# Linear attention followed by a SoLU layer: the leftover keys of two heads in row tiles, key sums and numerators in two shared banks

## The chip, the cores and the metric

The kernel runs on one core of one Trainium2 chip. The metric is the device time of one execution in microseconds, lower is better; a comparison uses the median of several runs. PE is the matrix engine, DVE, ACT and POOL the vector, scalar and GpSimd engines, SP the queue that issues all DMAs here.

## What is computed

Eight batches of eight heads, 576 tokens each, head width 64, go through a linear attention with 256 features; the 512 columns of the eight heads then go through a layer with a softmax gate and a layer norm.

```python
def phi(x):                                   # w_phi is 64 x 128
    proj = np.einsum('bhsd,df->bhsf', x, w_phi)
    proj = proj - np.max(np.abs(proj), axis=-1, keepdims=True)
    return np.concatenate([np.exp(proj), np.exp(-proj)], axis=-1)
q_p, k_p = phi(q), phi(k)
kv = np.einsum('bhsf,bhsd->bhfd', k_p, v)
z = np.sum(k_p, axis=2)
num = np.einsum('bhsf,bhfd->bhsd', q_p, kv)
den = np.einsum('bhsf,bhf->bhs', q_p, z)[..., None] + 1e-06
x = (num / den)                               # to 4608 rows of 512
h = x @ w_in                                  # 512 x 1024
e = np.exp(h - h.max(-1, keepdims=True)); solu = h * e / (e.sum(-1, keepdims=True) + 1e-9)
out = layer_norm(solu) * g_ln @ w_out         # 1024 x 512
```

## The kernel before

A unit `u` (16 of them) is four heads of one batch: two pairs, `sub` 0 and 1, of two heads `j` each. The host writes the keys and values of the two pairs one behind the other: 512 tokens of pair 0, its last 64, the last 64 of pair 1, 512 tokens of pair 1. So a unit has three groups `g` of token blocks of 128: four blocks of pair 0, one mixed block (`g` = 1, rows 0 to 63 belong to pair 0 and 64 to 127 to pair 1), four blocks of pair 1.

For the keys of a group, PE multiplies them with `w_phi` (`k_rows`, `k_mid`; tile pjk, both heads side by side as two row tiles of 64 rows), DVE takes the largest magnitude m and subtracts it, and ACT takes the exponentials of both signs `s` (tile ek, 128 tokens x 2 signs x 128 features). Unit 0 skips the subtraction on DVE: ACT takes the exponentials from PSUM, 128 columns at a time. Queries get their features fq in one of two ways; pjq, dT and pq are PE's part of that.

A visit (`visit`, one for each pair, V0 to V31) sums keys times values: for each head and sign it accumulates, over five blocks of tokens, ek (weights, split into two column tiles of 64 features) times the values rv with a column of ones, 65 columns. The fifth block is the mixed one, with the values of the other pair replaced by zeros (tile vz, cleared once by POOL, its halves loaded by `v_half_load`). All four sums stand in one PSUM bank; `kv_ev` copies them out (260 columns) to kvf. From the fifth visit on (`JOIN = 4`) PE runs the numerators of the previous pair, fq times kvf (`q_num`, 18 products in two column tiles for each sign), ahead of the key sums, into two banks of their own; `q_ev` copies these out with two instructions (390 and 195 columns) to E. For the first four pairs `q_num` is a step of its own. Then ACT, DVE, POOL and DVE again make the quotient y (rc, recip, `divide`, `x_turn`), and SP writes it to DRAM (dx).

The second part reads the quotients of a batch back (xT, from dx), splits them into high and low parts (ah by ACT, al and S by POOL) and runs Strassen-like products of 128x128 by 512 columns, U and h, then the gate, and the last product, o. It can start when the four pairs of batch 0, that is V0 to V4, are through. Its weights w_in and w_out come as 1 MB pieces wraw, which ACT (whi, the casts wb_h and wt_h, the scaling by g) and DVE (two instructions, the second joins the two halves) and POOL turn into high and low parts during the first 75 us.

The order of all steps is written out: `SEQUENCE` lists their numbers, and each engine executes its own in that order. PSUM has six banks of tag a, which everything here but h shares. A helper records each instruction, so all have line 275.

Of the kernel before, what the change touches and what calls it, by code (L numbers as in the profile page):

```python
# [8 lines left out]
F32 = mybir.dt.float32  # L9
# [22 lines left out]
JOIN = 4  # L32
# [10 lines left out]
    rk=3, rkm=2, rv=3, m=4, e=6, eh=2, kf=2, qr=2, qh=4, q4=2, m4=2, E=2, rc=2,  # L43
# [6 lines left out]
    ("rkm", 512), ("e", 5120), ("q4", 4608), ("qr", 2304), ("qh", 2304), ("E", 2376), ("kf", 1040),  # L50
# [236 lines left out]
def linear_attention_then_moe(ctx: ExitStack, tc, qT, qT2, kT, v, w_phi, w_in, g_ln, w_out, out):  # L287
# [51 lines left out]
    for t in v_half:  # L339
        nc.gpsimd.memset(t, 0.0)  # L340
# [279 lines left out]
    def visit(st, sub, before):  # L620

        kv = st["kv", sub] = bank("a", [P, 512], "kv")
        if before:
            q_num(*before)
# [132 lines left out]
    def q_ev(st, sub, i):  # L757
        if i == 0:
            st["E", sub] = sb("E", [P, 9, Z2], name="E")
# [585 lines left out]
```

## Time and profile before

| | us |
|---|---|
| median of 3 runs | 626.7 (625.62 to 628.13) |
| the profiled execution | 624.85 |
| its span, first to last instruction | 623.1 |
| PE busy | 610.3 (98%) |
| PE weight loads busy | 523.1 (84%) |
| DVE, ACT, POOL busy | 469.6, 460.7, 431.1 |

The granted clock of PE is full in every slice of the span. Matmuls overlap, so PE's busy time says where it works and not how fast; the distance from one start to the next does. DMA moves 166 GB/s on average, most in the first 30 us.

### The profile page before, as it was taken

The page shows a single profiled execution, that of the slowest core. Times are in us where ns is not written, and L with a number is a line of the kernel's source. Part 1 is how long each engine was busy: PE and PEld are TensorE (multiplying, and loading weights), DVE is VectorE, ACT ScalarE, POOL GpSimd, SP SyncE. Part 2 cuts the span into 40 slices and gives each one's busy share as a digit, 9 for nine tenths or more (in the row PEclk, how much of TensorE's full clock was granted, in tenths as well). Part 3 has the DMA queues.
Part 4 walks back from the last instruction along what each step waited for, and adds up shares of the span by engine and source line. Part 5 has one row for each costly group of instructions (what it writes and reads, how often), then busy time and mean ns, then how long its engine had stood idle before and what let it go on. Part 6 is the DMA issues. An engine that isn't in the chain of part 4 may idle for free.

```text
span 623.1 us, 19130 instructions
## 1 busy us (share of the span) xinstructions
PE 610.3 (98%) x7596; PEld 523.1 (84%) x7596; DVE 469.6 (75%) x1027; ACT 460.7 (74%) x872; POOL 431.1 (69%) x468
## 2 busy tenths in 40 slices
PE   7998999999999999999999999999999999999997
PEld 7887788888888888888888888888888888888886
DVE  5998899788779777887886699988878853454540
ACT  6998899588758977397686768787885685465662
POOL 0687898787659763867685676657886685586832
PEclk9999999999999999999999999999999999999999
DMA  8977435754557554636744455556543444456331
GB/s 273 362 232 234 122 124 164 212 148 138 173 152 180 170 188 150 177 86 181 229 157 131 155 163 183 174 169 179 168 139 107 139 153 126 126 144 201 125 133 69
DMA packets 100201, 103.33 MB, mean 166 GB/s; under 512 B 50448, under 2 KB 73232, under 8 KB 99600
## 3 DMA queue, kind: packets, MB, share of 16 engines
q1 hardware_dynamic: 100112, 102.11, 53.7%
q8 instruction: 60, 0.98, 0.7%
q14 instruction: 29, 0.24, 0.1%
HBM read 64.85 MB, written 37.22 MB: 164 GB/s over the span
## 4 chain that ended last, share of the span: by engine, by line
PE 92%; ACT 3%; POOL 1%; DMA 1%; issue 1%; DVE 1%; SPq 0%; ACTq 0%; POOLq 0%
PE o L275 32%; PE U L275 15%; PE h L275 12%; PE num L275 11%; PE kv L275 11%; PE pjk L275 6%; PE pq L275 4%; ACT ek L275 1%; DMA rawk<-in_k 1%; POOL al L275 1%; ACT fq L275 1%; PE dT L275 1%; ACT whi L275 0%; PE pjq L275 0%; POOL S L275 0%
## 5 line engine op out<-in xcount | busy, mean ns | idle before, releaser
L275 PE MATMUL o<-w_out_h,uhs 128*128 128x512 f32 x280 | 110.4, 394 | 0.0
L275 PE MATMUL o<-w_out_l,uhs 128*128 128x512 f32 x280 | 109.2, 390 | 0.0
L275 PE MATMUL o<-w_out_h,uls 128*128 128x512 f32 x280 | 109.0, 389 | 0.0
L275 POOL TENSOR_TENSOR uls<-uTs,uhs 128x1024 fp32r<-128x1024 f32 x35 | 83.7, 2390 | 35.6 <-ACT uhs L275 15.7
L275 ACT ACTIVATE ek<-ek 128x512 f32<-128x512 f32 (+1 forms) x150 | 86.7, 604 | 13.9 <-DVE ek L275 13.3
L275 PEld LDWEIGHTS num<-kvf,fq 128*64 128x64 f32 x2304 | 69.8, 137 | 9.5 <-issue 3.9
L275 PE MATMUL kv<-rv,ek 128*64 128x65 f32 x2048 | 76.6, 222 | 0.7 <-DMA rv<-in_v 0.5
L275 ACT ACTIVATE fq<-fq 128x640 f32<-128x640 f32 (+1 forms) x104 | 69.1, 678 | 7.5 <-DVE fq L275 7.1
L275 PE MATMUL num<-kvf,fq 128*64 128x65 f32 x2304 | 74.1, 222 | 0.0
L275 PEld LDWEIGHTS kv<-rv,ek 128*64 128x64 f32 x2048 | 70.8, 138 | 1.5 <-ACT ek L275 0.6
L275 POOL TENSOR_TENSOR blk<-blk,m 128x1152 f32<-128x1152 f32 x26 | 55.5, 2133 | 19.1 <-DVE m L275 19.1
L275 ACT ACTIVATE eu<-h,nm 128x1024 f32<-128x1024 f32 x36 | 40.2, 1117 | 37.7 <-DVE nm L275 29.0
L275 POOL TENSOR_TENSOR y<-E,rc 128x512 f32<-128x512 f32 x64 | 42.8, 690 | 32.6 <-DMA dx<-y 16.3
L275 POOL TENSOR_TENSOR al<-S,ah 128x512 fp32r<-128x512 f32 x36 | 46.8, 1300 | 26.8 <-ACT ah L275 26.6
L275 DVE SCALAR_TENSOR_TENSOR eu<-h,eu 128x1024 f32<-128x1024 f32 x36 | 43.6, 1211 | 25.6 <-ACT eu L275 22.7
L275 PEld LDWEIGHTS o<-w_out_h,uhs 128*128 128x128 f32 x280 | 52.5, 188 | 12.2 <-issue 0.4
L275 PEld LDWEIGHTS o<-w_out_h,uls 128*128 128x128 f32 x280 | 52.6, 188 | 11.1
L275 PEld LDWEIGHTS o<-w_out_l,uhs 128*128 128x128 f32 x280 | 52.6, 188 | 10.6
L275 DVE STREAM_TRANSPOSE blk<-pq 128x320 f32<-128x320 f32 (+1 forms) x104 | 44.5, 456 | 19.8 <-PE pq L275 19.6
L275 DVE TENSOR_REDUCE m<-pjk 128x4 f32<-128x512 f32 (+1 forms) x96 | 49.4, 541 | 10.5 <-PE pjk L275 10.1
L275 POOL TENSOR_TENSOR al<-xT,ah 128x512 fp32r<-128x512 f32 (+1 forms) x36 | 37.6, 1044 | 25.6 <-ACT ah L275 24.0
L275 DVE STREAM_TRANSPOSE ub<-eu 128x1024 f32<-128x1024 f32 x35 | 43.2, 1235 | 15.8 <-ACT eu L275 8.8
(116 smaller groups left out, 1561.6 us busy)
## 6 DMA issues: line engine op xcount, KB each, us to landing
du<-ub SPq DMA_DIRECT2D x35, 512.0 KB, 2.9
uTs<-du SPq DMA_DIRECT2D x140, 128.0 KB, 3.1
dx<-y SPq DMA_DIRECT2D x32, 288.0 KB, 2.4
out<-os SPq DMA_DIRECT2D x35, 256.0 KB, 3.1
rv<-in_v SPq DMA_DIRECT2D x32, 264.0 KB, 3.8
rawk<-in_k SPq DMA_DIRECT2D x32, 256.0 KB, 4.1
xT<-dx SPq DMA_DIRECT2D x64, 128.0 KB, 3.2
rawq<-in_q SPq DMA_DIRECT2D x26, 288.0 KB, 3.4
```

The lines of the kernel that those rows point to most:

```text
L275: return self.tc.keep_in_program_order(method(*args, **kwargs))
```

## The change

The host now writes the mixed block by heads instead of by pairs: for the keys, pair `sub` stands on rows 64 sub to 64 sub + 63 of the input and the two heads' 64 leftover tokens side by side, so that after `k_mid` rows 0 to 63 of ek are head 0 and rows 64 to 127 head 1, with the pairs in the two halves of the tile; the values likewise. A new step `visit_mid` (Vm, "the mid" below) multiplies them: for each sign two products, one for each head, in row tiles of 64 rows by 128 features, each head into a bank of its own. The padded tiles, their clearing and their second load are gone.

The visit itself takes up the two banks of its mid, has four blocks of tokens instead of five, and puts the numerators of the previous pair into the same two banks: half of them and head 0's sums into the first, the rest and head 1's sums into the second. Two copies (455 and 390 columns, tile KE) take the place of three; the first visit's copy 130 each. Every visit but the first takes numerators along; only the last pair's have a step of their own.

```diff
-JOIN = 4
...
+    def visit_mid(st, sub):
+        kv = st["kv", sub] = [bank("a", [P, 512], "kv") for _ in range(2)]
+        e, rv = st["kf", 1, None], st["rv", 1]
+        for s in range(2):
+            for j, r in enumerate(HEADS):
+                nc.tensor.matmul(
+                    block(kv[j], KV_AT[j] + s), lhsT=e[r, sub, s], rhs=rv[r, sub, :Z1], start=s == 0, stop=False,
+                    skip_group_check=True,
+                )
     def visit(st, sub, before):
-        kv = st["kv", sub] = bank("a", [P, 512], "kv")
-        if before:
-            q_num(*before)
+        kv = st["kv", sub]
         tiles = [(st["rv", 2 * sub][:, t], [st["kf", 2 * sub, j][:, t] for j in range(2)]) for t in range(4)]
-        tiles.append((st["vz"][:, sub], [st["kf", 1, None][:, j] for j in range(2)]))
         for j in range(2):
+            if before:
+                q_num(*before, kv, j, False)
             for s in range(2):
-                o = kv[:, (2 * j + s) * Z1 : (2 * j + s + 1) * Z1]
+                o = block(kv[j], KV_AT[j] + s)
                 for i, (rv, e) in enumerate(tiles):
                     for r in HEADS:
-                        nc.tensor.matmul(o[r], lhsT=e[j][:, s, r], rhs=rv[:, j, :Z1], start=i == 0, stop=i == 4)
+                        nc.tensor.matmul(
+                            o[r], lhsT=e[j][:, s, r], rhs=rv[:, j, :Z1], start=False, stop=i == 3,
+                            skip_group_check=True,
+                        )
...
-    def kv_ev(st, sub):
-        st["kvf", sub] = sb("kf", [P, 4, Z1], name="kvf")
-        nc.scalar.copy(out=st["kvf", sub].rearrange("p a f -> p (a f)"), in_=st["kv", sub][:, : 4 * Z1])
+    def visit_ev(st, sub, i, n):
+        if i == 0:
+            KE[n] = sb("KE", [P, sum(NB) * Z2], name="KE")
+        first, size = (0, NB[i]) if n else (KV_AT[i], 2)
+        evict(KE[n], KE_AT[i] + first, st["kv", sub][i], first, size)
...
+    kt[..., 512 : 512 + P] = k[..., 512:, :].transpose(0, 1, 2, 5, 3, 4).reshape(B, 2, P, P)
...
 SEQUENCE = (
-    0, 2, 110, 3, 177, 87, 90, 76, 88, 20, 180, 91, 181, 92, 78, 95, 93, 182, 94, 183, 83, 111, 79, 97, 112,
...
```

`SEQUENCE` is new throughout. Three places show it.

PE, the visit V14 of the kernel before, at 211.9 us of its trace. num and kv are column tiles, pjk and pq row tiles, o and h use the whole array; a count is of products.

```order
L275 MATMUL o<-w_out_h,uls 128x512
L275 MATMUL num<-kvf,fq 64x65 x36
L275 MATMUL kv<-rv_69,ek 64x65 x8
L275 MATMUL kv<-vz_71,ek 64x65 x2
L275 MATMUL kv<-rv_69,ek 64x65 x8
L275 MATMUL kv<-vz_71,ek 64x65 x2
...
L275 MATMUL pjk<-wph,rawk 128x128 x8
L275 MATMUL pq<-hq,w_hh 128x320 x2
```

The same engine in the new order, the visit V13 with its mid ahead and V14's mid behind it (kv<-vz is the mid, kv<-KE the numerators).

```order
L273 MATMUL U<-wt_h_623,al 128x512
L273 MATMUL kv<-vz_70,ek 128x65 x4
L273 MATMUL pq<-hq,w_hh 128x320 x2
L273 MATMUL pq<-hq,w_ll 128x320 x2
L273 MATMUL pq<-lq,w_hh 128x320 x2
L273 MATMUL kv<-KE,fq 64x65 x20
L273 MATMUL kv<-rv_68,ek 64x65 x16
L273 MATMUL kv<-KE,fq 64x65 x16
L273 MATMUL kv<-rv_68,ek 64x65 x16
L273 MATMUL kv<-vz_71,ek 128x65 x4
L273 MATMUL pq<-hq,w_hh 128x256 x2
```

The padded products have left the visit, numerators and key sums alternate by bank, and the mid stands with other row-tile products ahead of the visit that it belongs to.

SP at the start: the order before, as far as the first piece of w_in, then the new order's first six rows.

```order
L275 DMA rawq_148<-in_q 128x512
L275 DMA wph<-in_w_phi 128x128
L275 DMA rawk<-in_k 128x128 x2
L275 DMA rawk<-in_k 128x512
L275 DMA vz_70<-in_v 64x132
L275 DMA wraw_162<-in_w_in 128x2048
```

```order
L273 DMA wraw_137<-in_w_in 128x2048
L273 DMA rawk<-in_k 128x128
L273 DMA wph<-in_w_phi 128x128
L273 DMA rawk<-in_k 128x128
L273 DMA rawk<-in_k 128x512
L273 DMA rawq_185<-in_q 128x512
```

A piece of w_in, 1 MB, has moved from the seventh place to the first, ahead of the first keys and w_phi.

ACT at the start: the order before, as far as its first work on w_in, then the new one (m is the negated maximum, ek the exponentials of unit 0's keys).

```order
L275 ACTIVATE m<-m 128x2
L275 ACTIVATE ek<-pjk,m 128x128 x4
L275 ACTIVATE ek<-ek 128x2x128
L275 ACTIVATE m<-m 128x4
L275 ACTIVATE ek<-pjk,m 128x128 x4
L275 ACTIVATE m<-m 128x4
L275 ACTIVATE whi<-wraw_162 128x1024
```

```order
L273 ACTIVATE whi<-wraw_137 128x1024
L273 CAST wb_h<-w_3_141 128x1024
L273 ACTIVATE m<-m 128x2
L273 ACTIVATE ek<-pjk,m 128x128 x2
L273 ACTIVATE m<-m 128x4
```

The work on that piece now stands ahead of the first exponentials; wb_h waits for DVE, which has to join the halves first.

## Rows read from the trace of the kernel before

**Rows 1.** The page's head and part 1: busy us (share of the span) xinstructions.

```profile
span 623.1 us, 19130 instructions
...
PE 610.3 (98%) x7596; PEld 523.1 (84%) x7596; DVE 469.6 (75%) x1027; ACT 460.7 (74%) x872; POOL 431.1 (69%) x468
```

**Rows 2.** The page's part 4, the chain that ended last, by engine.

```profile
PE 92%; ACT 3%; POOL 1%; DMA 1%; issue 1%; DVE 1%; SPq 0%; ACTq 0%; POOLq 0%
```

**Rows 3.** Busy time by stage: us, each engine busy (xinstructions), clock, DMA share, GB/s.

```profile
8.50:49.70 41.20, 37.72 (x808) 33.90 (x806) 39.21 (x71) 40.66 (x110) 26.60 (x20) 1.00 0.86 299
49.70:66.60 16.90, 14.05 (x322) 12.47 (x319) 14.07 (x25) 14.49 (x30) 11.65 (x8) 1.00 0.76 216
66.60:618.90 552.30, 551.89 (x6433) 470.41 (x6431) 414.13 (x925) 401.94 (x725) 391.59 (x433) 1.00 0.52 154
```

**Rows 4.** Chain that ended last, 205 to 229 us: start us, us, what.

```profile
211.88 2.25 PE num L275 x72
214.13 2.33 PE kv L275 x80
216.46 1.09 PE pjk L275 x16
...
218.35 1.57 PE h L275 x6
...
225.36 1.36 PE h L275 x6
```

**Rows 5.** The same chain, 248 to 251 us.

```profile
249.20 0.89 PE pjk L275 x16
```

**Rows 6.** Timeline of weight loads, windows 211.79:211.895 and 216.385:216.48: start, us, engine, what.

```profile
211.81 0.20 PEld L275 LDWEIGHTS num<-kvf,fq 128*64 128x64 f32 x4 [0.35 <-ACT ek L275]
...
216.39 0.19 PEld L275 LDWEIGHTS pjk<-wph,rawk 64*128 64x128 f32 x2
```

**Rows 7.** Timeline of all engines, 201.0 to 201.5 us.

```profile
201.07 0.19 PEld L275 LDWEIGHTS pq<-hq,w_hh 64*128 64x128 f32 x2
201.08 0.38 PE L275 MATMUL pq<-hq,w_hh 64*128 64x256 f32 x2
201.18 0.19 PEld L275 LDWEIGHTS pq<-hq,w_ll 64*128 64x128 f32 x2
201.30 0.28 PE L275 MATMUL pq<-hq,w_ll 64*128 64x256 f32 x2
```

**Rows 8.** Timeline of all engines at the start.

```profile
0.72 0.39 SPq L275 DMA_DIRECT2D rawq<-in_q  x1
...
6.13 0.20 ACT L275 ACTIVATE m<-m 128x2 f32<-128x2 f32 x1 [4.13 <-DVE m L275]
...
8.50 0.20 ACT L275 ACTIVATE m<-m 128x4 f32<-128x4 f32 x1 [0.69 <-DVE m L275]
...
9.85 1.11 ACT L275 ACTIVATE whi<-wraw 128x1024 f32<-128x1024 f32 x1
...
15.92 1.21 DVE L275 SCALAR_TENSOR_TENSOR w<-whi,w 128x1024 uint32<-128x1024 uint32 x1
...
18.79 1.17 ACT L275 CAST wb_h<-w 128x1024 fp32r<-128x1024 f32 x1
```

**Rows 9.** DMAs of tile wraw, issue to landing, us.

```profile
DMA to landing us min/median/max: 5.6/7.0/10.9
```

**Rows 10.** Timeline of all engines ahead of the first U.

```profile
62.79 0.68 ACT L275 CAST ah<-xT 128x512 fp32r<-128x512 f32 x1
...
63.66 1.34 ACT L275 ACTIVATE w<-w,gcol 128x512 f32<-128x512 f32 x2
...
66.62 0.47 PE L275 MATMUL U<-wb_h,ah 128*128 128x512 f32 x1
```

**Rows 11.** Groups of ACT's instructions: busy us, mean ns.

```profile
L275 ACT COPY E<-num 128x390 f32<-128x390 f32 x32 | 16.3, 509 | 15.5 <-PE num L275 13.8 <-POOL sa L275 1.4
...
L275 ACT COPY E<-num 128x195 f32<-128x195 f32 x32 | 11.2, 349 | 1.7 <-PE num L275 1.5
```

More of the change, by code (lines that the diff above doesn't have):

```diff
@@ L315, in linear_attention_then_moe @@
     v_full = [const.tile([P, 4, 2, Z2], F32, name=f"rv{i}") for i in range(NRV)]
-    v_half = [const.tile([P, 2, 2, Z2], F32, name=f"vz{i}") for i in range(NVZ)]
+    v_mid = [const.tile([P, 2, Z2], F32, name=f"vz{i}") for i in range(NVZ)]
     wph = const.tile([P, F], F32, name="wph")
@@ L532, in v_load, with v_mid_load @@
         nc.sync.dma_start(out=rv[:, :nt], in_=v[st["b"], st["qd"], :, t0 : t0 + nt])
[L534 to L538 removed]
+    def v_mid_load(st):
+        vm = st["rv", 1] = v_mid[plan.slot[st["u"], "rv", 1]]
+        nc.sync.dma_start(out=vm, in_=v[st["b"], st["qd"], :, 4])
     def two_banks(name):
@@ L618, in k_exp_direct, with block, blocks @@
                 )
+    KV_AT, NUM_AT, KE_AT, NB = (0, 4), (2, 0), (0, 7), (7, 6)
+    def block(x, i):
+        return x[:, i * Z2 : i * Z2 + Z1]
+    def blocks(x, i, n):
+        return x[:, i * Z2 : (i + n) * Z2].rearrange("p (b f) -> p b f", f=Z2)
+    def visit_mid(st, sub):
[7 more added lines that the diff above has]
+                )
@@ new lines, in evict, with kv_of, num_of @@
+    def evict(out, o, x, i, n):
+        nc.scalar.copy(out=blocks(out, o, n)[:, :, :Z1], in_=blocks(x, i, n)[:, :, :Z1])
+    KE = {}
+    def visit_ev(st, sub, i, n):
[3 more added lines that the diff above has]
+        evict(KE[n], KE_AT[i] + first, st["kv", sub][i], first, size)
+    def kv_of(n, j, s):
+        return block(KE[n], KE_AT[j] + KV_AT[j] + s)
+    def num_of(n):
+        return blocks(KE[n + 1], NUM_AT[0], 9)
@@ L736, in q_exp, with q_num @@
         nc.scalar.activation(out=f[:, :, s], in_=f[:, :, 1], func=AF.Exp, scale=1.0 - 2.0 * s)
-    def q_num(st, sub):
-        odd, kvf = st["b"] % 2, st["kvf", sub]
-        po = st["num", sub] = [bank("a", [P, 512], "num") for _ in range(2)]
+    def q_num(st, sub, po, half, first):
+        odd, n = st["b"] % 2, 2 * st["u"] + sub
         lone = 0 if odd else 8
@@ L748, in run, with last_num, last_ev @@
                     f = st["qf", sub, c][:, j, s, k * D - Q0[c] : (k + 1) * D - Q0[c]]
-                    nc.tensor.matmul(o[HEADS[h]], lhsT=f, rhs=kvf[:, 2 * j + s], start=s == 0, stop=s == 1)
-        for p in range(4):
-            for j in range(2):
-                i = 2 * (p % 3) + j
-                run([(2 * p + odd + h, j, h) for h in range(2)], po[p // 3][:, i * Z2 : i * Z2 + Z1])
-        run([(lone, h, h) for h in range(2)], po[1][:, 2 * Z2 : 2 * Z2 + Z1])
-    def q_ev(st, sub, i):
+                    nc.tensor.matmul(
+                        o[HEADS[h]], lhsT=f, rhs=kv_of(n, j, s), start=first and s == 0, stop=s == 1,
+                        skip_group_check=True,
+                    )
+        todo = [[(2 * p + odd + h, j, h) for h in range(2)] for p in (2 * half, 2 * half + 1) for j in range(2)]
+        if half == 0:
+            todo.insert(0, [(lone, h, h) for h in range(2)])
+        for i, b in enumerate(todo):
+            run(b, block(po[half], NUM_AT[half] + i))
+    def last_num(st, sub):
+        po = st["num"] = [bank("a", [P, 512], "num") for _ in range(2)]
+        for half in range(2):
+            q_num(st, sub, po, half, True)
+    def last_ev(st, i, n):
         if i == 0:
-            st["E", sub] = sb("E", [P, 9, Z2], name="E")
-        n = 6 - 3 * i
-        out = st["E", sub][:, 6 * i : 6 * i + n, :Z1]
-        nc.scalar.copy(out=out, in_=st["num", sub][i][:, : n * Z2].rearrange("p (b f) -> p b f", b=n)[:, :, :Z1])
+            KE[n] = sb("KE", [P, sum(NB) * Z2], name="KE")
+        evict(KE[n], KE_AT[i] + NUM_AT[i], st["num"][i], NUM_AT[i], 5 - i)
     def den_eps(st, sub):
         st["rc", sub] = sb("rc", [P, NBLK], name="rc")
-        den = st["E", sub][:, :, 32:33].to_broadcast([P, 9, 2])
+        den = num_of(2 * st["u"] + sub)[:, :, 32:33].to_broadcast([P, 9, 2])
         nc.scalar.activation(
@@ L776, in divide @@
     def divide(st, sub):
-        e, rc = st["E", sub].rearrange("p b (h f) -> p (b h) f", h=2)[:, :, :32], st["rc", sub]
+        e, rc = num_of(2 * st["u"] + sub).rearrange("p b (h f) -> p (b h) f", h=2)[:, :, :32], st["rc", sub]
         y = st["y", sub] = sb("y", [P, S], name="y")
-        for n, o, h in ((slice(0, 16), y[:, :512], 4), (slice(16, 18), y[:, 512:], 2)):
+        for n, o, h in ((slice(2, 18), y[:, :512], 4), (slice(0, 2), y[:, 512:], 2)):
             nc.gpsimd.tensor_tensor(
@@ L800, in keys_values @@
     def keys_values(n):
-        return [(n // 2, "kve", n % 2)]
+        return [(n // 2, "kve", n % 2, i) for i in range(2)]
     def features(n):
@@ L831, in linear_attention_then_moe @@
             else:
-                for i in range(2):
-                    add(("vl", g, i), "sync", dma(n * 256), z - 3.5, v_half_load, (i,), [("vl", g, 0)] if i else [("abs", "vz")],
-                        () if i else [("vz", ("rv", g))], [("rv", g)])
+                add(("vl", g), "sync", dma(n * 512), z - 3.5, v_mid_load, (), (), [("vz", ("rv", g))])
             add(("kp", g), "tensor", 224 if g == 1 else 4 * 224, z, k_mid if g == 1 else k_rows,
@@ L854, in linear_attention_then_moe @@
             n = 2 * u + sub
-            joined = n >= JOIN
             z = 4.0 + 4.5 * sub
-            cost = 20 * BLOCK
+            cost = 16 * BLOCK
             pu, ps_ = (n - 1) // 2, (n - 1) % 2
-            feats = [(2 * sub, 0), (2 * sub, 1), (1, None)]
-            after = [("ke", *x, 1) for x in feats] + [("vl", 2 * sub), ("vl", 1, 1)]
-            tiles = [("e", *x) for x in feats] + [("rv", 2 * sub), ("rv", 1)]
-            alloc, early = [("a", ("kv", sub))], {}
-            if joined:
+            feats = [(2 * sub, 0), (2 * sub, 1)]
+            both = [("kv", sub, i) for i in range(2)]
+            add(("Vm", sub), "tensor", 2 * BLOCK, z, visit_mid, (sub,), [("ke", 1, None, 1), ("vl", 1)],
+                [("a", x) for x in both], [("e", 1, None), ("rv", 1)])
+            after = [("Vm", sub)] + [("ke", *x, 1) for x in feats] + [("vl", 2 * sub)]
+            tiles = [("e", *x) for x in feats] + [("rv", 2 * sub)] + both
+            early = {(u, "kve", sub, 0): 16 * BLOCK / 2}
+            if n:
                 after += [("abs", x) for x in features(n - 1)] + [("abs", x) for x in keys_values(n - 1)]
-                tiles += [("abs", (pu, "f", ps_, c)) for c in range(2)] + [("abs", (pu, "kf", ps_))]
-                alloc += [("a", ("abs", (pu, "num", ps_, c))) for c in range(2)]
-                early = {(pu, "qv", ps_, c): cost + 6 * BLOCK * (1 - c) for c in range(2)}
+                tiles += [("abs", (pu, "f", ps_, c)) for c in range(2)] + [("abs", ("KE", n - 1))]
+                early = {(u, "kve", sub, 0): 16 * BLOCK}
                 cost += 18 * BLOCK
-            add(("V", sub), "tensor", cost, z, visit, (sub, (states[pu], ps_) if joined else None), after, alloc, tiles,
-                early)
-            add(("kve", sub), "scalar", act(4 * Z1, True), z, kv_ev, (sub,), [("V", sub)], [("kf", ("kf", sub))],
-                [("kv", sub)])
+            add(("V", sub), "tensor", cost, z, visit, (sub, (states[pu], ps_) if n else None), after, (), tiles, early)
+            for i in range(2):
+                add(("kve", sub, i), "scalar", act(460 - 66 * i, True), z, visit_ev, (sub, i, n),
+                    [("V", sub)] + ([("kve", sub, 0)] if i else []), () if i else [("KE", ("abs", ("KE", n)))],
+                    [both[i], ("abs", ("KE", n))])
         if not qsp:
```

40 lines of the change are left out of this document (16 added, 24 removed), and 270 rows, old and new, of the table SEQUENCE.

## The prediction

> **What bounds the kernel now.** I read the page first: of a span of 623.1 us PE is busy 610.3 [rows 1]. Busy PE is no proof that PE is the bound, so the chain that ended last came next: 92% of it is PE, 3% ACT [rows 2]. The busy time by stage then says where that holds [rows 3]. From 66.6 to 618.9 us PE lacks 0.4 us of 552, while DVE, ACT and POOL have 130 us and more to spare: there only what PE executes counts. Ahead of 66.6 us it is another kernel: ACT lacks 0.5 us of 41 between 8.5 and 49.7, and PE stands still for 3.5.
>
> So the change is worth what it takes from PE's stream after 66.6 us, plus what it does to the time of the first U matmul, 66.62 us. The profiled execution took 624.85 us, 1.75 over its span; the median of the runs is 626.7. I add the difference to both.
>
> **PE's prices.** Every fp32 product is two instructions on each of two tiles side by side; I call what two tiles do together a pass. Three forms of the array occur: whole (128\*128: o, U, h, dT), column tiles (128\*64: num, kv), row tiles (64\*128: pjk, pjq, pq). From the chain around the visit at 211.9 us [rows 4]:
> - column tiles: kv x80, 40 passes in 2.33 us, 0.058 each;
> - row tiles, 128 columns streamed: 8 passes in 0.89 us where row tiles ran before them [rows 5], 0.111 each;
> - a change of form: the same pjk x16 take 1.09 behind column tiles, so 0.20 to enter row tiles; h x6 take 1.57 behind row tiles and 1.36 in a run of its own form, 0.21 to enter the whole array; num x72 take 2.25, of which 36 passes are 2.10, 0.15 to enter column tiles [rows 4, 5].
>
> **The leftover keys.** Each of the 32 visits now spends 8 of its 40 kv passes on the padded fifth block: 8 x 0.058 = 0.466 us. The mid puts four products there, two per sign, head 0 on rows 0 to 63 and head 1 on rows 64 to 127: 4 passes. The price of such a pass is in no row: it streams 65 columns as kv does, but loads weights of 128 columns as pjk does. Its ends are 0.058 (streaming limits) and 0.16 (a load of 0.11 and a stream of 0.05, half of pjk's, one after the other). What decides is the weight load. Right behind a change of form, four loads of 64 columns begin within 0.085 us, but only two of 128 columns within 0.09 [rows 6]; and in pq, entered from another form, the second pair of loads starts 0.11 after the first, and the second pair of matmuls 0.22 after the first, a load and a stream of 0.11 each [rows 7]. So a pair of 64x128 loads takes about 0.11 us and a 64-column load half of that. In kv load and stream are equally long, in pjk too; in the mid the stream is halved and the load is not. I take 0.111: 4 x 0.111 = 0.444 us instead of 0.466, 32 x -0.022 = -0.7 us. The ends: 32 x (0.234 - 0.466) = -7.4 and 32 x (0.64 - 0.466) = +5.6 us.
>
> The page "TensorEngine Tiling (Array Packing)" of the Trainium skill, section Theoretical Speedup, gives a contraction of at most 64 a factor of up to two; the mid by it would be the -7.4.
>
> **Changes of form.** Counted over PE's whole order, before against now: into the whole array 43 and 43, into column tiles 35 and 33, into row tiles 44 and 57. Half the mids (16) follow a product of the whole array and precede another row-tile group, as in the order shown above: there the visit, entered from the whole array before, now is entered from row tiles, and what followed it has to be entered all the same. Cost: 13 x 0.20 - 2 x 0.15 = +2.3 us. Nine mids stand right ahead of another form; their last pass ends after 65 columns, not 128: 9 x -0.05 = -0.5. Nothing hides these, since PE is the bound.
>
> **Evictions and banks.** Three evictions of 260, 390 and 195 columns become two of 455 and 390. The rows have 0.51 us for 390 and 0.35 for 195 [rows 11], so 0.16 per 195 columns: 0.40 + 0.51 + 0.35 before, 0.56 + 0.51 now, 0.19 us of ACT less a visit. ACT has 150 us free in that stage [rows 3]: nothing. Without that cover it would be 32 x 0.19 in favour. A visit holds two banks of six instead of three, but from the mid on; PE waits nowhere for a bank after 66.6 us, so nothing, either way. Numerators now wait for the key sums that share their bank, up to 2.3 us longer; behind them stand only the divisions, whose output is wanted a batch later. The first batch is the exception, and belongs to the start. Sixteen fewer DMAs on SP's queue and no clearing of padded tiles on POOL: nothing, neither stands in the chain.
>
> **The start.** Ahead of the first U, PE executes the same numbers of pjk, pjq, pq, num and kv products, 24 mids for 48 padded products and six more dT: at the prices above 51.5 us against 51.7. U starts at 66.62, so 15 us are lost there now, to ACT's queue mostly. That queue is rearranged: the first DMA becomes 1 MB of w_in, and whi and the cast of wb_h stand ahead of every exponential. It is issued at about 0.72 us, where rawq is now; the eight 1 MB pieces land 5.6 to 10.9 us after their issue [rows 8, 9]. Nothing is queued ahead of this one, so I take 6: landed at 6.7, whi 1.0, DVE's join 1.2, wb_h 0.95, and the exponentials begin at 9.9. By then ACT has done 3.1 us of work in the kernel before (from 6.13, less 0.69 of idling [rows 8]), and 2.0 in the new one: 1.1 behind. Ahead of the first ah stand four multiplications by g (two take 1.34 [rows 10]), one exponential less, three evictions less: about 1.8 more. Against that ACT idles 2.4 us between 49.7 and 66.6 [rows 3]. The first ah, at 62.79 [rows 10], moves by 1.1 + 1.8 - 2.4 = 0.5, and the POOL work on w_in starts earlier. The last numerators of the first batch now leave PE at their visit's end, up to 2.3 us later, and division, transpose and DMA have that much less until the first ah; some of what they have now is spent in ACT's queue, where ah waits its turn. I take the start as even, with bounds of -2 (the 2.4 of idle ACT gone) and +4.5 (below).
>
> **Sum.** -0.7 + 2.3 - 0.5 + 0 = +1.1 us: a span of 624.2, an execution of 626.0, and 626.7 + 1.1 = **627.8 us** for the median. By its own bounds, the start's, this case lies between 625 and 630.
>
> **The rivals.**
> 1. The mid's passes are limited by streaming, 0.058 each: -7.4 + 2.3 - 0.5 = -5.6, 621.1 us. For it: kv runs at that price. Against it: the loads [rows 6, 7]. 17%.
> 2. The 1 MB at the head of the queues delays the start, and the result is slower. Place: ACT's first instruction, behind which all exponentials wait, and pjk's keys, which travel behind the same megabyte. Price: landing after 10.9 us rather than 6 shifts the exponentials from 9.9 to 14.8; ACT, gapless from there, passes on all but what its idle time takes: about +4.5, 632 us. It decides from a landing at about 8 us. For it: the median of the eight pieces is 7.0 [rows 9], and ACT is gapless [rows 3]. Against it: this piece has the queue to itself. 18%.
> 3. The new order loses less ahead of U: ACT used from 6.7 us on and its 2.4 us of idling gone, -3 with the POOL work that starts earlier: 624.8, at best a little under 623.6. 9%.
> 4. A weight load waits until the matmul of the same rows is through: +5.6 + 1.8 = +7.4, 634 us. Against it: pjk passes of 0.111 with a load of 0.11 in each leave no room for it [rows 5]. The page "TensorE: Matmul & The Clock Gate" of the Trainium skill, Part 3, The mechanism, says that LDWEIGHTS overlaps with running matmuls only when the row group differs; by that rule it would be this rival, and the pjk row speaks against the rule. 3%.
>
> **How the numbers follow.** The likeliest case has 53%. Half a per cent, 3.1 us, is about what a measurement of this kernel can tell from no change: faster means under 623.6, slower over 629.8. Faster: rival 1 (17) and the better part of rival 3 (3), 20%. Slower: rival 2 (17), rival 4 (3), and the upper edge of the likeliest case (4), 24%. The same: 56%. The range takes in rivals 1 and 2, 621 to 632.
>
> **What would show it.** In the chain after: mids of x8 in about 0.44 us (0.23: rival 1; 0.65: rival 4), and 1.09-like entries ahead of them. In the stages: PE without idle time from the first U on; first U at 66 to 67 us (71: rival 2; 64: rival 3). PE's busy groups of num and kv unchanged per pass. The prediction is wrong if PE waits for ACT's evictions or banks after the first U, or if a change of form between mid and visit costs other than 0.15 to 0.21.

## The result and the profile after

The changed kernel takes 632.2 us (631.76 to 633.5, four runs) against 626.7 for the kernel before: a ratio of 1.009, 95% interval 1.0064 to 1.0115. It is slower, by 5.5 us; 627.8 had been forecast, with a range of 621 to 632. The profiled execution took 631.97 us, its span is 6.3 us longer than the one before.

First the page's head, part 1 and the engines of the chain, which answer to [rows 1, 2].

```profile
span 629.4 us, 18547 instructions
...
PE 615.1 (98%) x7340; PEld 525.4 (83%) x7340; DVE 470.2 (75%) x1027; ACT 459.0 (73%) x842; POOL 429.6 (68%) x466
...
PE 90%; DVE 4%; POOL 2%; DMA 1%; ACT 1%; issue 1%; SPq 0%; POOLq 0%; ACTq 0%
```

PE is busy 4.8 us longer in a span 6.3 us longer, and of the chain DVE now has 4% and POOL 2%, where each had 1%. The busy time by stage, cut as in [rows 3], with the first U at 69.54 instead of 66.62 us:

```profile
8.50:49.70 41.20, 37.62 (x738) 34.35 (x736) 34.88 (x63) 39.95 (x113) 22.83 (x16) 1.00 0.77 265
49.70:66.60 16.90, 15.22 (x298) 13.94 (x300) 15.92 (x32) 14.65 (x28) 12.30 (x9) 0.90 0.75 219
66.60:69.54 2.94, 2.94 (x73) 2.87 (x69) 2.94 (x5) 2.42 (x5) 1.92 (x2) 1.00 0.95 199
69.54:625.20 555.66, 554.23 (x6219) 469.49 (x6217) 413.76 (x925) 398.31 (x696) 391.81 (x433) 1.00 0.51 154
```

So the time went to two places: 2.9 us ahead of the first U, and 3.4 us behind it (552.2 before, 555.6 now, from the start of the first U to the end of the last product). The second stage also has a granted clock of 0.90, where it was 1.00.

**Behind the first U.** PE lacked 0.4 us there and lacks 1.4 now. What it waits for in the whole execution, longest first (us in total, times, longest):

```profile
PE pjk L273 <- DMA rawk<-in_k: 2.4, 1, 2.4
PE U L273 <- POOL al L273: 1.4, 2, 0.8
PE pjk L273 <- DVE dq L273: 1.3, 1, 1.3
PE pq L273 <- ACT fq L273: 1.2, 2, 0.7
...
```

Only the second of these lies behind the first U. With the slow first products after each stop, the U, h and o products take 1.8 us more than before. The rest, +1.6 us, is PE's own work, counted from start to start over all its instructions: the distances across a change of form +3.25 (96 of them before, 111 now, each with the last product of the old form in it, so this is not yet their price), the products of padded block, mid and key sums together -0.82 (59.33 to 58.51), transposes dT that moved ahead of the first U -0.49, pjk, pq and numerators -0.3.

The chain shows a visit and its mid as [rows 4, 5] showed them before (start us, us, what):

```profile
246.05 0.59 PE kv L273 x8
246.64 0.40 PE pq L273 x6
247.05 4.12 PE kv L273 x136
...
292.16 1.09 PE pjk L273 x16
293.26 0.39 PE kv L273 x8
293.65 0.28 PE pjk L273 x4
```

The visit is 36 passes of numerators and 32 of key sums in 4.12 us, 0.0606 a pass with its change of form, where 76 passes took 4.58, 0.0603, before [rows 4]. The mid's four passes take 0.39 between other row tiles, and 0.59 behind the whole array: 0.20 to enter row tiles, as forecast. And two copies of 0.54 and 0.49 us stand in place of the three of [rows 11]; PE waits for none of them (x, busy us, mean ns):

```profile
L273 ACT COPY KE<-kv 128x455 f32<-128x455 f32 x31 | 16.7, 538 | 18.1 <-PE kv L273 17.5 <-POOL y L273 0.5
L273 ACT COPY KE<-kv 128x390 f32<-128x390 f32 x31 | 15.1, 485 | 14.2 <-PE kv L273 14.0
```

**Ahead of the first U.** Timeline of ACT at the very start, to be held against [rows 8]: the megabyte of w_in has landed by 5.5 us, 4.8 after its issue, and the exponentials begin at 9.1.

```profile
5.52 1.11 ACT L273 ACTIVATE whi<-wraw 128x1024 f32<-128x1024 f32 x1 [3.52 <-DMA wraw<-in_w_in]
7.92 1.04 ACT L273 CAST wb_h<-w 128x1024 fp32r<-128x1024 f32 x1 [1.29 <-DVE w L273]
...
9.10 0.37 ACT L273 ACTIVATE ek<-pjk,m 128x128 f32<-128x128 f32 x1
```

PE's work, each product at the price of its kind, gives how far PE was at a time: by 8.5 us it had done 3.3 us of it before and has 2.4 now, by 20 us 10.2 and 8.9, by 57.5 us 40.3 and 39.9, by 61 us 42.7 and 40.8, by 65 us 45.3 and 43.0. These prices leave changes of form out. So PE has nearly made up its late beginning by 57.5 us, and loses 2.0 us in the 7.5 that follow; 0.5 is the dT work that now stands ahead of U. 0.4 + 2.0 + 0.5 is the 2.9 of the first U. PE's timeline there:

```profile
57.25 0.60 PE L273 MATMUL dT<-ident,dq 128*128 128x128 f32 x4
58.51 0.41 PE L273 MATMUL pq<-hq,w_hh 64*128 64x320 f32 x1 [0.66 <-ACT fq L273]
59.44 0.41 PE L273 MATMUL pq<-hq,w_hh 64*128 64x320 f32 x1 [0.52 <-ACT fq L273]
...
60.69 0.94 PE L273 MATMUL pjq<-wph,rawq 64*128 64x128 f32 x12 [0.42 <-DVE ek L273]
```

Three stops, and behind them the granted clock falls to its lower level, 0.50 or 1.2 GHz, from 62 to 65 us (columns as in [rows 3]):

```profile
57.50:61.00 3.50, 1.90 (x16) 1.24 (x15) 3.50 (x6) 3.50 (x10) 3.50 (x2) 1.00 0.88 308
61.00:62.00 1.00, 1.00 (x17) 0.94 (x15) 1.00 (x4) 1.00 (x3) 1.00 (x2) 0.81 0.27 78
62.00:65.00 3.00, 3.00 (x43) 2.88 (x43) 3.00 (x3) 2.05 (x3) 2.01 (x1) 0.50 0.98 217
```

The same stretches before:

```profile
57.50:61.00 3.50, 3.32 (x60) 2.85 (x62) 2.74 (x4) 3.50 (x9) 2.51 (x2) 1.00 0.90 201
61.00:62.00 1.00, 1.00 (x42) 1.00 (x40) 1.00 (x3) 1.00 (x3) 0.00 (x0) 1.00 0.92 322
62.00:65.00 3.00, 1.87 (x64) 1.73 (x61) 2.96 (x5) 2.92 (x7) 1.45 (x1) 1.00 1.03 234
```

So the stops alone don't make the difference: in these 7.5 us PE is idle 1.60 us now and 1.31 before, and from 8.5 us to the first U 5.3 now and 6.3 before.

Meanwhile the operands of the first U come later too. POOL's last division of batch 0 starts at 55.65 us, 4.2 later than before (51.43): its numerators start 2.0 us later on PE (50.11 instead of 48.06) and leave it with V4's key sums, so that the last copy behind them starts at 54.34 instead of 50.43. SP issues the quotient (dx) at 57.81 instead of 53.86, and reads it back (xT) from 60.58 on instead of 56.03. On POOL:

```profile
51.05 1.32 POOL L273 TENSOR_TENSOR y<-KE,rc 128x512 f32<-128x512 f32 x2 [1.35 <-DMA dx<-y]
...
55.65 1.32 POOL L273 TENSOR_TENSOR y<-KE,rc 128x512 f32<-128x512 f32 x2 [0.66 <-DVE rc L273]
56.93 7.08 POOL L273 TENSOR_TENSOR wt_l<-w,wt_h 128x1024 fp32r<-128x1024 f32 x3
67.62 1.67 POOL L273 TENSOR_TENSOR S<-xT 128x256 f32<-128x256 f32 x1 [3.60 <-DMA xT<-dx]
69.25 1.72 POOL L273 TENSOR_TENSOR al<-xT,ah 128x512 fp32r<-128x512 f32 x1
```

ACT's first ah starts at 67.56; it was 62.79 [rows 10]. It waits for the read to land, not for its turn in ACT's queue:

```profile
67.56 0.93 ACT L273 CAST ah<-xT 128x512 fp32r<-128x512 f32 x2 [0.52 <-DMA xT<-dx]
```

POOL's order adds to it: an S of 1.67 us now stands ahead of the first al, where before al came first and S at 65.85. No run puts that back.

```profile
63.55 2.34 POOL L275 TENSOR_TENSOR al<-xT,ah 128x512 fp32r<-128x512 f32 x1 [3.54 <-ACT ah L275]
```

So two chains end within 1.5 us of each other: PE's own, at 69.54, and the operands', which makes PE stop twice right behind (71.02 and 74.71, for al).

### The profile page after: what moved, and what is told of

Same layout as the page of the kernel before. It is cut to its first block, busy times and chain, and to the rows that moved or that the text cites. A ratio compares the mean times of both kernels' runs of the same rounds, so it can differ in the third digit from the quotient of the medians.

```text
span 629.4 us, 18547 instructions
## 1 busy us (share of the span) xinstructions
PE 615.1 (98%) x7340; PEld 525.4 (83%) x7340; DVE 470.2 (75%) x1027; ACT 459.0 (73%) x842; POOL 429.6 (68%) x466
## 4 chain that ended last, share of the span: by engine, by line
PE 90%; DVE 4%; POOL 2%; DMA 1%; ACT 1%; issue 1%; SPq 0%; POOLq 0%; ACTq 0%
PE o L273 32%; PE kv L273 20%; PE U L273 16%; PE h L273 12%; PE pjk L273 5%; PE pq L273 4%; DVE m L273 1%; ACT ek L273 1%; PE pjq L273 1%; DMA rawk<-in_k 1%; POOL S L273 1%; DVE w L273 1%; POOL y L273 1%; DVE ek L273 1%; DVE dq L273 1%
## 5 line engine op out<-in xcount | busy, mean ns | idle before, releaser
L273 ACT ACTIVATE ek<-ek 128x512 f32<-128x512 f32 (+1 forms) x150 | 85.2, 587 | 17.9 <-DVE ek L273 17.1
L273 PE MATMUL kv<-KE,fq 128*64 128x65 f32 x2232 | 78.0, 224 | 0.0
L273 PEld LDWEIGHTS kv<-KE,fq 128*64 128x64 f32 x2232 | 71.0, 139 | 5.3 <-issue 2.5
L273 PE MATMUL kv<-rv,ek 128*64 128x65 f32 x2048 | 70.5, 222 | 0.0
L273 POOL TENSOR_TENSOR y<-KE,rc 128x512 f32<-128x512 f32 x64 | 43.2, 697 | 38.4 <-DVE rc L273 28.6
L273 PEld LDWEIGHTS kv<-rv,ek 128*64 128x64 f32 x2048 | 65.2, 138 | 0.1
L273 ACT COPY KE<-kv 128x455 f32<-128x455 f32 (+1 forms) x64 | 32.4, 509 | 32.3 <-PE kv L273 31.5
```

Source lines behind the costliest of these rows:

```text
L273: return self.tc.keep_in_program_order(method(*args, **kwargs))
```

## The experiments

Two theories of the prediction were to be tested: that the mid is limited by its weight loads, and that the start comes out even. The second having fallen, the candidates for what moved the start are called here: **A**, the late last quotient; **B**, the megabyte at the head of the queues (the prediction's rival 2); **C**, PE's stops and its clock; **D**, transfers that travel with the quotient; **E**, ACT's work on w_out ahead of the first ah. Steps moved in `SEQUENCE` are given by name.

### The mid's price: its products twice

```diff
+        for s in range(2):
+            for j, r in enumerate(HEADS):
+                nc.tensor.matmul(
+                    block(kv[j], KV_AT[j] + s), lhsT=e[r, sub, s], rhs=rv[r, sub, :Z1], start=False, stop=False,
+                    skip_group_check=True,
+                )
```

> The changed kernel with the four products of each mid done a second time (so the leftover keys count twice in the sums): 4 passes more in each of 32 visits, no change of form more. If the load of 128 columns limits a pass (0.10 to 0.111 us): 128 passes, 12.8 to 14.2 us more, 645 to 646.4. If streaming limits it (0.058): 7.4 more, 639.6. If a load waits for the matmul on its rows (0.16): 20 more, 652.7.

646.1 us (643.84 to 650.41), 13.9 above the changed kernel, or 13.3 by the ratios to the kernel before (1.0302 and 1.009): 128 passes more, 0.104 to 0.109 each. In its chain the mid between the same neighbours as above:

```profile
303.70 1.09 PE pjk L273 x16
304.79 0.84 PE kv L273 x16
305.63 0.28 PE pjk L273 x4
```

0.84 - 0.39 = 0.45 for four passes, 0.112 each. A pass costs what one of pjk costs, which streams 128 columns, though only 65 stream here: rival 1 (0.058) and rival 4 (0.16) are both out. What the two have in common is the load of 128 columns; that it is the load, and not the form as such, is argued, since no run loads fewer columns into row tiles. By the Trainium skill, page "TensorEngine Tiling (Array Packing)", section Theoretical Speedup, two row tiles give up to twice the speed; here the mid, 0.44 us, costs what the padded passes cost, 0.47, so the trace doesn't show that factor. By the page "TensorE: Matmul & The Clock Gate" of the Trainium skill, Part 3, The mechanism, a weight load overlaps with running products only in another row group; that would have been 0.16, and the trace disagrees.

### The price of a change of form: each mid in two halves

One half of the mid (the products of the negative sign) moves into the middle of its visit, between the two banks: no pass more, two changes of form more in each of 32 visits.

```diff
-        for s in range(2):
-            for j, r in enumerate(HEADS):
...
+        mid_half(st, sub, 0)
...
         for j in range(2):
+            if j == 1:
+                mid_half(st, sub, 1)
             if before:
```

> The changed kernel with two of each mid's four passes (the second sign) moved into the middle of its visit, between the sums of head 0 and the numerators of the second bank: the same products, but 64 changes of form more, 32 into row tiles and 32 into column tiles. If a change costs 0.20 and 0.15 us and nothing hides it: 32 x 0.35 = 11.2 us more, 642 to 645. If a change costs nothing by itself (the 0.2 being waits of another kind): 632 to 634.

641.5 us (639.54 to 642.84), 1.0226 of the kernel before [1.0199 to 1.0253]: 8.8 us above the changed kernel on the same chip (632.65), 0.14 for each of 64 changes. Its chain:

```profile
249.84 0.37 PE kv L273 x4
250.21 0.40 PE pq L273 x6
250.61 4.64 PE kv L273 x140
```

A visit takes 4.64 instead of 4.12, its mid 0.37 instead of 0.59: +0.30 for two changes. The 0.20 + 0.15 of the prediction would be 0.35, but it also takes off 0.05 where a mid stands right ahead of another form, as this half does: 0.30, as measured. What was expected of this run left that out.

The starts show where this time goes (means over the 207 changes of both kernels behind the first U, beside the same passes in a run). The first pass of a new form starts 0.09 to 0.10 us late, whichever form is left and whichever comes. The second pass is late again: 0.05 us in column tiles and in a mid, 0.10 in pjk and pq, 0.11 in o, U and h. Together that is 0.14 to 0.15 into column tiles, 0.20 into pjk and pq, 0.21 into the whole array: the price goes by the form that is entered, as the prediction had it. Into a mid it is 0.14, and the pjk or pq behind that mid then comes 0.05 late, which makes 0.20 again. In the changed kernel, from o into pq (0.31 to the first pass and 0.25 to the second, where 0.23 and 0.15 are usual in a run):

```profile
263.44 0.39 PE L273 MATMUL o<-w_out_h,uls 128*128 128x512 f32 x1
263.75 0.41 PE L273 MATMUL pq<-hq,w_hh 64*128 64x320 f32 x2
264.00 0.31 PE L273 MATMUL pq<-hq,w_ll 64*128 64x320 f32 x2
264.15 0.31 PE L273 MATMUL pq<-lq,w_hh 64*128 64x320 f32 x2
```

### Fewer changes of form, other orders: three misses

Twelve groups of PE products moved by at most 28 places of the list, so that like forms meet (96 changes instead of 111 behind the first U); the changed products in the order of the kernel before; and that order with each mid behind its visit. The first by a list of moves, the other two by another `SEQUENCE`; in the last the visit also takes up and starts the banks, and its mid ends the sums.

```diff
+MOVES = (
+    (2271, 2228),
+    (1761, 1787),
+    (1518, 528),
+    (1519, 528),
+    (1180, 1271),
...
+SEQUENCE = moved(SEQUENCE, MOVES)
```

> The changed kernel with twelve groups of steps moved on PE by up to 40 places of the list, so that behind the first U the array changes its form 96 times, as in the kernel before, instead of 111. What each product executes and the start up to the first U are unchanged. If a change of form costs 0.15 to 0.21 us and nothing hides it, 15 fewer take off 2.3 to 3.2 us: 629.0 to 629.9. The rival, that what is lost behind the first U lies in the mids or in waits: within 0.7 us of 632.2.

> The changed products (mids, joined visits, two shared banks) in the order of the kernel before: each step stands where it stood there; the mid of a visit stands right ahead of it, or beside an earlier row-tile group where banks allow; visit V1, which now takes the numerators of pair 0, stands where these stood. Changes of form: 139 in all, 115 behind the first U (before 122 and 96, changed kernel 133 and 111). Theory O (the 4 us ahead of and around the first U are the new order's): first U at 66.5 to 68, the start as before, and behind it 19 more changes of form than before, at 0.15 to 0.21 each, less about 1.2 for the mids: 626.8 + 2.6, 628.5 to 630.5 us. Theory J (they belong to the joined visits and the mids themselves): first U at 69 to 71 here too, 632 to 634.

> The order of the kernel before again, now with each mid right behind its visit instead of ahead of it (the visit takes the two banks and starts them, the mid closes the sums, the copies wait for it). In that order a visit is mostly followed by another row-tile group, so the mid needs no change of form of its own: 122 in all, 98 behind the first U, as before. Theory (only the number of changes of form and the order ahead of U cost time): the start as before (first U at 66.5 to 68), and less than the kernel before by what a mid saves, 0.02 to 0.07 in 32 visits: 624.5 to 626.3 us. Rival: the copies, 0.4 us later in each visit, hold up the next numerators or the banks: 627.5 or more, with waits of PE for ACT's copies behind the first U.

699.6, 683.9 and 694.2 us, 9 to 12% slower. What PE waits for in the first:

```profile
PE pq L308 <- DVE ek L308: 6.2, 4, 2.1
PE pjk L308 <- DVE ek L308: 5.6, 2, 3.2
PE pq L308 <- DVE m L308: 5.0, 2, 2.6
PE kv L308 <- ACT fq L308: 4.6, 2, 3.2
...
```

Moved products run into operands and banks that aren't ready, 1.5 to 3 us each time, though DVE and ACT have over 130 us to spare. None of the three tells the price of a change of form. What they show is that these moves on PE alone don't do, and that the order of before doesn't carry the new products, so whether the new order as such costs the time can't be tested by going back to it.

### The start: megabyte, clock, quotients

B: the megabyte of w_in, its split and join, back behind the first keys and exponentials. C: repeated products (six each of a dT, a pq and a pjq step) in the three stops. A: the four quotients of batch 0 earlier, the last pair's numerators again in a step of their own ahead of V4. And A with C. (The diffs show a part of each edit.)

```diff
+    (19, 93),
+    (20, 80),
+    (57, 12),
+    (21, 100),
+    (22, 13),
+    (58, 59),
```

> The changed kernel with one thing undone: the first megabyte of w_in, and the ACT, DVE and POOL work on it (whi, the two DVE instructions, wb_h, wb_l), stand where they stood before, behind the first keys and the first exponentials. Theory A (the start is lost at the last quotient of batch 0, whose DMA moved from 53.9 to 57.8 us, and which the first U products need): that DMA stays within 1 us of 57.8, the third U product within 1 us of 71.0, the time within 1 us of 632.2. Theory B (the megabyte at the head of the queues, because of which the first keys are multiplied at 6.38 instead of 4.81 us): everything behind moves up by 1.6 us or more, the time to 628.0 to 630.6.

```diff
-            nc.tensor.transpose(out=pt[:, c0 : c0 + P], in_=d, identity=ident)
+            for _ in range(6 if (st["u"], sub, c, j) == FILL[0] else 1):
+                nc.tensor.transpose(out=pt[:, c0 : c0 + P], in_=d, identity=ident)
```

> The changed kernel with idempotent repeats of products (three transposes six times, a pq and a pjq product six times more) in the stretch from 57.8 to 60.7 us where PE waits three times, 1.6 us in all, before its granted clock falls to 0.50 for some 3.6 us (61.4 to 65.0). If the fall follows from the waits, the clock is 1.00 throughout and the products there take half their time. Theory A (the last quotient, and behind it POOL's al, sets when U can go on): first U 1.0 to 1.8 us earlier (67.7 to 68.5 instead of 69.5), but the third U product, the first that needs al, still at 71.0 within 0.4, and the time within 0.5 us of 632.2. Theory C (the lost clock is what the start costs): the time falls by 1.7 us to about 630.5.

```diff
+ALONE = 4
...
+    op((u, "qo"), "tensor", 18 * BLOCK, 0, last_num, (states[u], sub), features(n) + keys_values(n),
```

> The changed kernel with the quotients of batch 0 made earlier, in two ways at once: pair 0's reciprocal, division and transpose stand ahead of pair 1's, when its sums have been there for 8 us (the one buffer of y makes the four pairs go one behind the other, 4.6 to 5.7 us each), and the numerators of the last pair of batch 0 are a step of their own again, ahead of the mid and visit of unit 2, with their own two banks and copies, so that they don't wait for that visit's key sums. Theory A: the last quotient's DMA goes from 57.8 to 55.3 to 56.0 us, the first xT and al come 2 us earlier, U's waits for al (0.77 and 0.62 us) go; then PE's own chain, with half the clock from 61.4 to 65.0, is the bound and first U stays at 69.0 to 69.6: 1.2 to 1.9 us less, 630.3 to 631.0. Theories B and C (the megabyte, the clock alone): within 0.5 us of 632.2.

> The two preceding edits together: early quotients and the repeats that keep PE's clock up. Theory A, by which the two chains end within 1.5 us of one another: now the clock counts too, first U at 67.5 to 68.2 without a wait for al of over 0.4 us, and 2.8 to 3.6 us less, 628.6 to 629.4: more than the sum of what each gives alone. Theory C: only what the clock gives alone, 1.7 us.

634.1, 633.3, 633.0 and 633.4 us (ratios 1.012, 1.0096, 1.0101, 1.0104, each within 0.0022): none is faster than the changed kernel. With the megabyte put back the first U is at 70.2, no earlier. The test isn't clean, since the granted clock was low in the stretch that follows, where the changed kernel had 1.00; but B promised 1.6 to 4.2 us, and the megabyte's landing after 4.8 us, far under the 8 from which rival 2 decides, speaks against it by itself, as does PE's lag of 0.4 us at 57.5 us.

```profile
8.50:20.00 11.50, 7.83 (x96) 7.48 (x98) 7.83 (x13) 9.84 (x38) 0.00 (x0) 0.59 1.03 392
```

In C the clock was 1.00 from 61 to 65 us, but the repeats filled more than the stops (first U at 70.2). In A the last quotient left only 0.3 us earlier (57.55), since its reciprocal and transpose stood late in DVE's queue, and POOL's al waited 3.3 us for ah, which stood behind V5's copy in ACT's. That test isn't clean either: the granted clock was 0.50 from 61 to 65 us.

### The start again, with more loosened at once

The changed kernel again on another chip; it with ten warming products instead of six and the repeats; the earlier quotients on top, with DVE's and ACT's steps moved too.

```diff
-NWARM = 6
+NWARM = 10
...
+    (245, 291),
+    (246, 289),
...
+    (247, 294),
...
+    (284, 67),
```

> The changed kernel itself, as the ground for its variants on the same chip. Every theory: 631.5 to 633.5 us, the first U at 69 to 72, depending on where PE's granted clock falls in the start.

> The changed kernel with the repeats alone, at both places, so PE's clock stays up through the start. Theory A: first U up to 1.8 us earlier, but the products that need al wait as long as before: within 0.6 us of the changed kernel on the same chip. Theory C (the clock is what the start costs): 1.5 to 2 us less.

> The changed kernel with all that theory A puts on the path to the first U made earlier at once: the quotients as in the third experiment, with the last pair's reciprocal and transpose placed two DVE steps earlier; the conversions ah ahead of the copy of V5's sums on ACT; and repeats of products that keep PE busy where it waits at 4.0 to 6.4 and 57.8 to 60.7 us. Theory A (the last quotient and what follows it cost the start its 4 us, the clock the next 1.7): last quotient's DMA at 55.5 to 56.3 (57.8 in the changed kernel), ah at 64 to 65.5 (67.6), first U at 67.4 to 68.3 with at most 0.5 us of waits for al behind it, 628.4 to 629.6 us. If the start is bound elsewhere: within 1 us of the changed kernel.

632.7, 631.2 and 631.3 us. The filled stops and the ten warming products together are worth 1.5 us, and the clock stays up (as in the rows of after, 62 to 65 us):

```profile
62.00:65.00 3.00, 3.00 (x68) 2.93 (x68) 2.14 (x4) 3.00 (x5) 2.48 (x2) 1.00 0.67 149
```

The earlier quotients give nothing more: the last one was issued at 55.53, 2.3 us earlier, but landed 5.3 us after its issue, not 2.6. Hence D: the last megabyte of w_out, issued at 53.6, moved to 29.7 us; the ten warming products alone; both with lighter repeats; and all of it with the earlier quotients.

```diff
+    (33, 161),
```

> The changed kernel with one DMA moved: the last megabyte of w_out, which SP issues at 53.6 us, right ahead of the last quotient's DMA and of the reads xT, is issued at 29.7 us instead, where SP then waits for the first quotient. Theory D (the transfers of the start share the DMA engines, and this piece delays the quotient's landing and xT, which took up to 5.5 us): xT lands at 65 to 66.5 instead of 67.6 us, al follows, and 0.7 to 1.5 us less than the changed kernel's 632.6: 631 to 632. If the transfers don't matter: within 0.5 us of 632.6.

> The changed kernel with ten products to warm up PE instead of six, so that it works until the first keys land at 6.4 us instead of stopping at 4.0. With the repeats at both places the time was 1.5 us less, with those at 57.8 us alone about the same. If the clock at the start is what counts: 631.0 to 631.6; if the repeats at 57.8 us are needed too: 632 to 633.

> The changed kernel with the last megabyte of w_out early, ten products to warm up, and repeats at 57.8 to 60.7 us that fill PE's waits without delaying what follows (about 1.7 us of them instead of 2.9). Theory: the clock (1.5 us) and the transfers (0.7 to 1.5) add up, since each is a term of the same chain: 629.6 to 630.6 us, first U at 68 to 69. If POOL's work on w_in sets xT's buffer free too late: 631 as with the repeats alone.

> The same with the early quotients of the eleventh run: there the last quotient left at 55.5 us but took 5.3 us to land, and xT started no earlier. With the megabyte out of its way it should land in 2.5 us, xT start at 58.2 to 59 and land by 64, first U be bound by PE alone at 67.5 to 68.3 without a wait for al: 628.3 to 629.5 us, all of the start's loss but half a microsecond; what is left against the kernel before is then the changes of form. If the DMA stays slow: 630 to 631.

632.0, 632.8, 632.3 and 631.2 us, ratios 1.0068, 1.0077, 1.0072 and 1.0052 [1.0034 to 1.007]. The last one's interval still overlaps that of the changed kernel measured again (1.009 [1.0067 to 1.0114]). The traces side by side: first U, the sum of PE's waits for operands right behind it, both together, and the rest from there to the end of the last product:

| kernel | first U | waits | both | rest | clock, 61 to 65 us |
|---|---|---|---|---|---|
| before | 66.6 | 0.3 | 66.9 | 551.9 | 1.00 |
| after | 69.5 | 1.4 | 70.9 | 554.2 | 0.58 |
| after, again | 70.4 | 1.0 | 71.5 | 554.6 | 0.67 |
| filled | 69.4 | 1.3 | 70.7 | 553.9 | 1.00 |
| w_out early | 68.6 | 2.1 | 70.7 | 554.9 | 1.00 |
| warm | 68.5 | 2.1 | 70.6 | 556.2 | 1.00 |
| w_out early, filled | 69.1 | 2.1 | 71.2 | 554.9 | 1.00 |
| early quotients, filled | 69.5 | 0.7 | 70.2 | 553.4 | 1.00 |
| all of it | 69.6 | 0.0 | 69.6 | 555.6 | 1.00 |

The two chains trade places. Where PE comes 1 us earlier (w_out early and warm: in these two profiles the clock didn't fall, though PE had the same stops), it waits longer for al. Where the operands come earlier, PE's own work is last, the repeats in it: in the last row the quotient lands 2.1 us after its issue, as D has it, ah starts at 65.58, and U still comes at 69.6. That each chain hides what is done to the other fits all rows, but two profiles of the same kernel differ by 0.5 us in the sum, and the rest varies by 2.8 us among the variants, 0.8 of it waits in warm, 0.5 in all of it, the others not traced: a gain of 1 us at the first U can't be priced from one profile.

### ACT's work on w_out

E: three passes over pieces of w_out, two pairs of multiplications by g and a cast, by their rows 7 us of ACT's queue between 49 and 69 us, moved behind the first ah; in the changed kernel, and on top of all the rest.

```diff
+    (39, 1402),
+    (27, 1402),
+    (34, 1402),
+    (29, 353),
+    (41, 31),
+    (42, 1404),
+    (67, 1404),
```

> Changed kernel, with ACT's work on w_out that stands ahead of the first ah (two casts of whole pieces, two pairs of multiplications by g, one cast to w_out_h: about 6 us between 49 and 69 us) moved behind it, into ACT's wait for POOL's S at 70.3 to 72.7 and after. Theory that the four multiplications ahead of ah and their companions cost the start (the prediction's +1.8, too small): PE's waits for fq at 58.5 and 59.4 go, first U at 67 to 68, no wait for al, median 628 to 629.5. Theory that the start is lost elsewhere (one y buffer, DMA and POOL for the quotients, DVE for the features): first U stays at 68.5 to 70, median 631.5 to 633.

> e16 (early quotients, filled waits, ten warming products, the last megabyte of w_out early) with the same ACT work moved behind the first ah as in e17. Theory of several chains that end together, ACT's among them: this is the first version that loosens all of them, first U at 67 to 68, no wait for al, median 628 to 629.5, at best the time before. Theory that ACT has no part in it: as e16, 631 to 632.

637.7 and 636.2 us, slower still. In the first, ACT idles ahead of ah, waiting for PE, and PE's stops are where they were:

```profile
58.02 0.41 PE L294 MATMUL pq<-hq,w_hh 64*128 64x320 f32 x1 [0.66 <-ACT fq L294]
58.95 0.41 PE L294 MATMUL pq<-hq,w_hh 64*128 64x320 f32 x1 [0.52 <-ACT fq L294]
...
66.21 0.54 ACT L294 COPY KE<-kv 128x455 f32<-128x455 f32 x1 [4.56 <-PE kv L294]
```

First U at 69.24, where it was 69.54: ACT's load isn't what holds it. The stops are a round trip, dT on PE, fq on ACT, the bank back to PE, with nothing else in PE's queue meanwhile. And the work moved came back as 3.7 us of PE waiting for ah, at 73.8 and 79.9, more than ACT's idle 2.4 us there could take in.

## Why the prediction was wrong, step by step

- **What bounds.** Right: PE-bound behind the first U (it lacks 1.4 us of 555.7, all of it in the first six), another kernel ahead of it.
- **The mid, -0.7.** Right in size, 0.104 to 0.112 a pass; that the load is what limits it is argued.
- **Changes of form, +2.3 - 0.5.** Right, in kind and in size. The prices go by the form that is entered, 0.20 into row tiles, 0.14 to 0.15 into column tiles, 0.21 into the whole array, and the split mid costs the 0.30 that they give. For the 15 changes that are more behind the first U (14 into row tiles, one into the whole array, four mids ahead of another form) they give 2.8 + 0.21 - 0.2 = +2.8; by the starts it is +2.0 at the changes, +1.2 in the groups behind a mid and -0.4 inside mids that follow row tiles.
- **The steady part together.** +1.1 forecast for the whole order, +1.6 measured behind the first U, where the same prices give 2.8 for the changes, -0.6 for 26 mids and -0.5 for the dT that moved ahead: 1.7.
- **Evictions and banks.** Right: PE waits for no copy and no bank.
- **The megabyte.** The landing was 4.8 us, not 6, and the exponentials began at 9.1 instead of 9.9. Rival 2 has the right size, 632, by luck as far as the runs show: the megabyte landed early, PE's lag was down to 0.4 us by 57.5, and with it put back the kernel is no faster (ratio 1.012, though at a low clock early on).
- **The start as even.** This step failed: 0 was taken, +4.7 came (2.9 at the first U, 1.8 behind it; its bounds ended at +4.5). It failed at the sentence "the first ah ... moves by 1.1 + 1.8 - 2.4 = 0.5". That sum is of ACT's queue alone, and ACT wasn't last there: ah moved by 4.8. The next sentence saw the cause, numerators up to 2.3 us later, and then charged it to ACT's queue without following it on. Followed, it was 4.2 us at the last division, as the numerators start 2.0 us later and come out bank by bank with the key sums of the next visit; the quotient's transfer and the read of xT then set ah. And I took the 15 us that PE loses ahead of U to stay the same by counting its work alone: from 8.5 us on its idle time there fell by 1 us, but some three us at half the clock came in, which no term of the sum had.

What stays open: no edit brought the first U with its operands below 69.6 us, against 66.9 before, so the two chains are shown but not the order that would shorten both, nor which step of either costs how much. Of the 2.0 us that PE loses between 57.5 and 65 us, about 1.2 go with the clock: in the two profiles with the same stops and a clock of 1.00 (w_out early, warm) it does 4.3 us of work there instead of 3.1, and 5.1 before. The first U came 1.0 us earlier in them, and the ratios, 1.0068 and 1.0077, are not clearly below 1.009.

## What to carry to other kernels

A term taken as "even" needs the same working as any other: follow each late result through every queue and buffer to the product that waits for it, not through the busiest engine alone. Where two chains end together, an edit to one shows little; list both ends, first product and waits behind it, before judging it, and the same kernel twice. And price a row-tile product by its weight load when fewer columns stream than are loaded: taking the padding out of a contraction gained 0.02 us a visit here and paid for it in changes of form.

## What was not expected of the hardware

A change of form costs twice, 0.09 to 0.10 us ahead of the first pass and 0.05 to 0.11 ahead of the second, and only the second part depends on the form that is entered. The granted clock fell to 0.50 for three us behind stops of 0.66, 0.52 and 0.42 us with work between them, and in two other profiles of the same PE order it didn't; in the kernel before, stops of 1.29 and 1.13 us at 55.7 and 64.0 us left it at 1.00. And one transfer of 288 KB took 2.6 us from issue to landing in one kernel and 5.3 in another that issued it 2.3 us earlier.
